# Reading the guard's flag behind the last store, and sending three of 24 stores in halves

## The chip, the core and the metric

The kernel runs on one core of a Trainium2 chip. The core has five engines with an instruction queue each: TensorE (PE, with its weight loads shown as PEld), VectorE (DVE), ScalarE (ACT), GpSimd (POOL) and SyncE (SP), which here issues all transfers. The metric is the time of one execution on the device in microseconds, taken from several runs by their median. The profile shows a single execution; its span goes from the first to the last instruction.

## What is computed

A gated linear attention over 4 batches, 8 heads, 768 positions and heads of 48, and a gated feed-forward part whose gate mixes the positions:

```python
f = 1 / (1 + exp(-f_logit))
for t in range(S):
    state = f[:, :, t, :, None] * state + einsum('bhd,bhe->bhde', k[:, :, t], v[:, :, t])
    y[:, :, t] = einsum('bhd,bhde->bhe', q[:, :, t], state)
x = y.transpose(0, 2, 1, 3).reshape(B, S, H * D)      # 4 x 768 x 384
h = gelu_tanh(x @ w_in)                               # 384 -> 1024
u, v = h[..., :512], h[..., 512:]
v_n = (v - mean) / sqrt(var + 1e-6) * g_ln
v_s = einsum('ts,bsd->btd', w_sg, v_n) + b_sg[None, :, None]
out = x + (u * v_s) @ w_out
```

All is float32. The result has 3072 rows of 384 numbers.

## The kernel before

The 3072 rows are cut into 24 tiles of 128 rows, six to a batch. For each tile the attention is computed in chunks of 64 positions, with the state carried along; then the tile goes through the first product, the GELU and the norm. The position mixing (`sgu`) runs over groups of three tiles, and behind it comes the product with `w_out` (`proj`), a residual addition on DVE (`residual`, L914) into a buffer of the ring `tmp`, and the store of the tile (`store`, L917), 128 rows of 1536 bytes.

A planner (`Plan.run`) puts all these steps into one order, from costs, due times and a list of shifts (`MOVES`), and the steps are then written out in this order under a manual schedule (L1169 to L1178). Each engine works through its own queue in that order. All transfers are issued by SP: the loads of f, k, q and v for a tile, the round trips through DRAM by which k and q are turned (`kq_d`, `raw`) and by which the decay goes to another layout (`dec_d`, `dec`), and the 24 stores. An issue that must wait holds up all that SP has behind it.

The transfers report through eight semaphores, which the framework hands out in rotation: each transfer takes the next, and is issued only when the one that had this semaphore eight transfers earlier has landed.

The fast path holds only for usual data. So the kernel collects flags (`guard`, `guard_sum`, `guard_end`), and a number `slow_i` says in the end whether a general path must run. Behind the last step every engine reads `slow_i` into a register (L1184) and branches (L1187). The general path is long, and is not entered with the data used here. Behind the branch stands a join, where SP waits for the eight semaphores of the transfers one after the other in a fixed order, and then the program closes (shown as L1283). At the step `ok_e`, L1178 marks a place for a branch hint on SP.

`store` is also called from the general path, where `row0` is a loop's register and not `None`.

Of the kernel before, what the change touches and what calls it, by code (L numbers as in the profile page):

```python
# [17 lines left out]
P = 128  # L18
C = 64
# [386 lines left out]
def gla_moe_kernel(ctx: ExitStack, tc: tile.TileContext, q, k, v, f, w_in, g_ln, w_sg, b_sg, w_out, cst, out):  # L406
    nc = tc.nc
# [72 lines left out]
    row0 = None  # L480
# [303 lines left out]
    out_flat = out.rearrange("b s e -> (b s) e")  # L784

    def out_rows(n):
        r = n * P if row0 is None else row0 + n * P
        return out_flat[ds(r, P), :]
# [121 lines left out]
    o_sb = {}  # L910
# [3 lines left out]
        nc.vector.tensor_add(o_sb[n], psum[f"po{n}"][:, :E], x_sb.pop(n))  # L914

    def store(n):
        nc.sync.dma_start(out_rows(n), o_sb.pop(n))  # L917

    slow_i = cp.tile([1, 1], mybir.dt.int32, name="slow_i")
    ok_t = {}  # L920
    last_sb = {}

    def guard():
        NG = 2 * N + N * 2 * NP
# [131 lines left out]
    for n in range(N):  # L1056
# [88 lines left out]
        if done:  # L1145
            plan.by[f"po{n}"]["needs"] += [f"po{n - 1}", f"po{n - 2}"]
        op(f"re{n}", lambda e, n=n: residual(n), T["re"], [f"po{n}"], take=("tmp",), unbank=f"po{n}", free=[("x", f"ty{n}", 0)])
        dma(f"out{n}", lambda e, n=n: store(n), W["out"], [f"re{n}"], free=[("tmp", f"re{n}", 0)])
    for n in range(NT, N):
        if n % NT == 0:  # L1150
# [30 lines left out]


    main.close()
    slow = nc.values_load(slow_i[0:1, 0:1], min_val=0, max_val=1)  # L1184

    table["set"] = "any"
    with tc.If(slow != 0, label="general"):  # L1187
# [27 lines left out]
        with tc.tile_pool(name="again", bufs=2) as wk, tc.tile_pool(name="ps_again", bufs=1, space=PSUM) as pp:  # L1215
# [4 lines left out]
            with tc.For_i(0, B * S, S) as row0:  # L1220
# [23 lines left out]
                for g in range(NT // GR):  # L1244
                    for ft in range(NF):
                        sums(f"sg{g}.{ft}")
                        sgu(g, ft)
                        sgu_bias(g, ft)
                        sgu_gate(g, ft, "POOL")
                        sgu_hi(g, ft)  # L1250
                        sgu_lo(g, ft)
                    for r in range(GR):
                        sums(f"po{g * GR + r}")
                        proj(g * GR + r)
                        residual(g * GR + r)
                        store(g * GR + r)
# [31 lines left out]
```

## Time and profile before

| | |
|---|---|
| median of 3 runs | 366.79 us (366.03 to 367.84) |
| the profiled execution | 365.51 us, span 363.7 us |
| mean granted TensorE clock | 0.997 |
| transfers | 45.89 MB, mean 126 GB/s |
| stores of results | 24, 192 KB each, all issued by SP |

The profiled execution is 1.28 us below the median of the three runs. In the rows of the profile a time such as 359.95 is counted from the start of the span. `SPq`, `PEldq` and the like are an engine's sequencer: waits, branches, register work and issues of transfers, which don't count as busy. For the issue of a transfer the row has the time that the issue took on SP, not the time until the data has landed. In a row of a line, "x4: 17/17/17, 360.8 to 361.1" is the count, the least, median and greatest duration in ns, and the start of the first and the last. In rows of waits the numbers are the total, the count and the longest, in us. In the table of stretches, the figures behind the stretch are its length, then the busy time (and count) of PE, PEld, DVE, ACT and POOL, the granted clock, the DMA share and GB/s.

### The profile page before, as it was taken

Reading aid. Unit: us, or ns where it says so; the run is one execution under the profiler, and the core shown is the slowest. Engines: PE = TensorE matmul, PEld = TensorE weight load, DVE = VectorE, ACT = ScalarE, POOL = GpSimd, SP = SyncE. Lnnn points to the kernel's source line nnn. Section 1 sums busy time; section 2 is a strip of 40 time slices with the busy share of each in tenths; the row PEclk is TensorE's granted clock in tenths of the full one; section 3 lists DMA queues with packets and bytes.
Section 4 is the critical chain, followed back from the end, with each engine's and each line's share of the span. In section 5 each row is a group of like instructions: output and inputs, shape, how many; then the busy total and the mean of one; then the engine's idle time right before and its main releaser. Section 6 shows DMA issues by size and latency. Waiting matters only on the chain.

```text
span 363.7 us, 11376 instructions
## 1 busy us (share of the span) xinstructions
PE 357.3 (98%) x4676; PEld 325.6 (90%) x4676; DVE 242.9 (67%) x561; ACT 241.0 (66%) x503; POOL 63.5 (17%) x113
## 2 busy tenths in 40 slices
PE   7999999999999999999999999999999999999995
PEld 3678788899999989899998999999998898999994
DVE  2999887788998966449765665255886944245532
ACT  5678999998658799798526674899424683811100
POOL 2211232322332201121002020130600010200100
PEclk9999999999999999999999999999999999999998
DMA  8999989425789778625744932035564720000012
GB/s 188 221 239 203 211 162 243 104 74 145 161 207 221 180 176 203 131 57 140 179 88 110 199 69 64 3 88 132 144 154 78 221 64 25 3 22 2 0 43 94
DMA packets 134046, 45.89 MB, mean 126 GB/s; under 512 B 117221, under 2 KB 130405, under 8 KB 133990
## 3 DMA queue, kind: packets, MB, share of 16 engines
q1 hardware_dynamic: 133990, 45.12, 53.3%
q8 instruction: 38, 0.62, 0.7%
q14 instruction: 18, 0.15, 0.1%
HBM read 33.25 MB, written 11.85 MB: 124 GB/s over the span
## 4 chain that ended last, share of the span: by engine, by line
PE 93%; DMA 3%; ACT 1%; SPq 1%; issue 0%; DVE 0%
PE ps_b L796 69%; PE ps_y L772 7%; PE ps_s L724 4%; PE ps_b L1168 3%; PE ps_s L729 2%; PE ps_b L801 2%; PE ps_b L679 2%; DMA cs<-in_consts_dram 2%; PE ps_b L664 1%; PE ps_b L627 1%; DMA vs<-in_v_dram 1%; PE ps_b L556 1%; PE ps_b L630 1%; PE ps_b L631 1%; SPq L500 0%
## 5 line engine op out<-in xcount | busy, mean ns | idle before, releaser
L796 PE MATMUL ps_b<-w_sg_hi,vh 128*128 128x384 f32 x192 | 65.6, 342 | 0.0
L796 PE MATMUL ps_b<-w_sg_hi,vh_lo 128*128 128x384 f32 x192 | 64.9, 338 | 0.0
L796 PE MATMUL ps_b<-w_sg_lo,vh 128*128 128x384 f32 x192 | 64.8, 338 | 0.0
L796 PE MATMUL ps_b<-w_out_hi,gg 128*128 128x384 f32 x174 | 48.3, 339 | 0.0
L428 ACT ACT_TABLE_LOAD x31 | 39.8, 1283 | 0.6
L796 PEld LDWEIGHTS ps_b<-w_sg_hi,vh 128*128 128x128 f32 x192 | 36.1, 188 | 0.2
L796 PEld LDWEIGHTS ps_b<-w_sg_lo,vh 128*128 128x128 f32 x192 | 36.1, 188 | 0.0
L796 PEld LDWEIGHTS ps_b<-w_sg_hi,vh_lo 128*128 128x128 f32 x192 | 36.0, 188 | 0.0
L796 PEld LDWEIGHTS ps_b<-w_out_hi,gg 128*128 128x128 f32 x174 | 31.7, 188 | 0.2
L883 DVE SCALAR_TENSOR_TENSOR tmp<-ps_b,cols,b_bc 128x384 f32<-128x384 f32 x32 | 19.6, 613 | 16.8 <-PE ps_b L796 16.7
L899 ACT CAST gg<-tmp 128x384 fp32r<-128x384 f32 x29 | 14.7, 512 | 24.0 <-DVE tmp L888 18.5
L796 PE MATMUL ps_b<-w_out_lo,gg 128*128 128x384 f32 x87 | 29.1, 335 | 0.0
L796 PE MATMUL ps_b<-xTh,w_in_hi 128*128 128x384 f32 x84 | 29.1, 347 | 0.0
L430 ACT ACTIVATE f<-f 128x384 f32<-128x384 f32 x48 | 25.3, 527 | 5.7 <-DMA f<-in_f_logit_dram 5.3
L856 DVE SCALAR_TENSOR_TENSOR vh_lo<-vg,vg_rs,vh 128x512 fp32r<-128x512 f32 x24 | 18.2, 759 | 15.4 <-ACT vh L851 15.2
L796 PE MATMUL ps_b<-xTh,w_in_lo 128*128 128x384 f32 x84 | 28.4, 338 | 0.0
L796 PE MATMUL ps_b<-xTl,w_in_hi 128*128 128x384 f32 x84 | 28.3, 337 | 0.0
L772 PEld LDWEIGHTS ps_y<-vs,st 64*64 64x64 f32 x768 | 24.5, 134 | 4.2 <-issue 3.6
L435 ACT COPY sk<-raw 112x512 f32<-112x512 f32 x27 | 16.2, 617 | 17.8 <-DMA raw<-kq_d 15.5
L772 PE MATMUL ps_y<-S,sk 48*64 48x48 f32 x768 | 27.2, 220 | 0.0
L772 PE MATMUL ps_y<-vs,st 64*64 64x48 f32 x768 | 27.2, 220 | 0.0
L796 PE MATMUL ps_b<-w_in_hi,xTh 128*128 128x512 f32 x63 | 25.7, 408 | 0.3 <-ACT u L430 0.2
(139 smaller groups left out, 883.9 us busy)
## 6 DMA issues: line engine op xcount, KB each, us to landing
kq_d<-gg SPq DMA_DIRECT2D x18, 384.0 KB
f<-in_f_logit_dram SPq DMA_DIRECT2D x24, 192.0 KB
kq<-in_q_dram SPq DMA_DIRECT2D x24, 192.0 KB
kq<-in_k_dram SPq DMA_DIRECT2D x24, 192.0 KB
vs<-in_v_dram SPq DMA_DIRECT2D x24, 192.0 KB
raw<-kq_d SPq DMA_DIRECT2D x36, 128.0 KB
out_dram<-tmp SPq DMA_DIRECT2D x24, 192.0 KB
gg<-in_moe_w_in_dram SPq DMA_DIRECT2D x8, 384.0 KB
```

What stands on the lines that cost most here:

```text
L428: nc.scalar.preload_act_table_set(SETS[want])
L430: nc.scalar.activation(dst, src, func, **kw)
L435: (nc.scalar.copy if e == "ACT" else ENG[e].tensor_copy)(dst, src)
L679: nc.tensor.transpose(psum[f"tr{n}"][j][:W2, p * P : (p + 1) * P], kq[:, j, 2 * p : 2 * p + 2, :].rearrange("t h d -> t (h d)")[:, :W2], i ...
L724: nc.tensor.matmul(ps_s[rows(score_rows(c, 2 * p + par)), par, p * C : (p + 1) * C], sk[r, 0, p, c], sk[r, 1, p, c], start=True, stop=True)
L729: nc.tensor.matmul(ps_s[feat(par), c, 256 + p * D : 256 + (p + 1) * D], kt[rows(c), h], vs[rows(c), h], start=True, stop=True)
L772: nc.tensor.matmul(ps_y[rows(c), half, h * D : (h + 1) * D], a, m, start=start, stop=stop)
L796: nc.tensor.matmul(ps, a, m, start=(j == 0), stop=(j == len(seq) - 1))
L856: nc.vector.scalar_tensor_tensor(vl, v_raw.pop(n), rs, vh.bitcast(F32), op0=ALU.mult, op1=ALU.subtract)
L883: nc.vector.scalar_tensor_tensor(t, psum[f"sg{g}.{ft}"][:, :E], g_col[:, ft : ft + 1], b_bc[:, tokens(g)], op0=ALU.mult, op1=ALU.add)
L899: nc.scalar.copy(gt[(g, ft)][0], g_raw[(g, ft)])
L1168: steps = plan.warm(plan.run(), 45.0, lambda k, n: nc.tensor.matmul(ps_b[k][:, : n * P], zeros, zeros[:, None, :].to_broadcast((P, n, P)), ...
```

## The change

Tiles 6, 7 and 8 are stored by two transfers of 64 rows each (`C` is 64), in place of one of 128 rows. All other stores stay, and the last one traced is kept in `last_store`. SP's instructions of the read of `slow_i` get an edge that orders them in SP's queue behind that store; it orders the issue and waits for no landing. The reads of the other engines are not touched.

```diff
     def store(n):
-        nc.sync.dma_start(out_rows(n), o_sb.pop(n))
+        o = o_sb.pop(n)
+        if row0 is None and n in (6, 7, 8):
+            nc.sync.dma_start(out_flat[n * P : n * P + C, :], o[:C])
+            nc.sync.dma_start(out_flat[n * P + C : (n + 1) * P, :], o[C:])
+        else:
+            last_store[0] = nc.sync.dma_start(out_rows(n), o)
...
-    last_sb = {}
+    last_sb, last_store = {}, [None]
...
     main.close()
-    slow = nc.values_load(slow_i[0:1, 0:1], min_val=0, max_val=1)
+    with tc.issue_after(last_store[0].ins):
+        slow = nc.values_load(slow_i[0:1, 0:1], min_val=0, max_val=1)
```

## Prediction

> **What bounds the kernel now.** I read the page first (span, busy times, chain), then the end of the run instruction by instruction: the timeline of SP, the chain of the last microseconds, and the views of lines 1184, 1187 and 1283, which hold the read of the flag, the branch with the join behind it, and the closing of the program. Last come the waits of SP, the stretches around the three split stores, and what PE waited for.
>
> ```profile
> span 363.7 us, 11376 instructions
> PE 357.3 (98%) x4676; PEld 325.6 (90%) x4676; DVE 242.9 (67%) x561; ACT 241.0 (66%) x503; POOL 63.5 (17%) x113
> PE 93%; DMA 3%; ACT 1%; SPq 1%; issue 0%; DVE 0%
> ```
>
> PE bounds the kernel up to its last product. The change adds no product and takes none away, so it can act in two places only: behind the last product, and where the extra store issues delay a load on which PE depends. The tail:
>
> ```profile
> 359.36 0.56 DVE tmp L914
> 356.10 0.33 SPq L917 DMA_DIRECT2D out_dram<-tmp  x1
> 357.83 0.34 SPq L917 DMA_DIRECT2D out_dram<-tmp  x1
> 359.95 0.33 SPq L917 DMA_DIRECT2D out_dram<-tmp  x1
> L1187 SPq COMPARE_BRANCH  x1: 70/70/70, 360.3 to 360.3; - x1
> L1187 SPq EVENT_SEMAPHORE  x4: 17/17/17, 360.8 to 361.1; - x4
> L1187 SPq EVENT_SEMAPHORE  x4: 17/17/17, 362.1 to 362.3; - x4
> SPq L1187 <- SPq L1187: 1.5, 2, 1.0
> L1283 SPq EVENT_SEMAPHORE  x8: 27/28/28, 362.4 to 362.9; - x8
> L1283 SPq DRAIN  x2: 7/10/13, 362.9 to 363.0; - x2
> L1283 PEldq DRAIN  x1: 8/8/8, 362.4 to 362.4; - x1
> ```
>
> The reader is to see one thread on SP. The last residual addition ends at 359.36 + 0.56 = 359.92; SP issues the last store at 359.95 and is free at 360.28; it branches at 360.3 and then waits for eight semaphores in turn. Four waits pass at once (360.8 to 361.1, so about 0.1 each). The fifth passes only at 362.1: this is the idle stretch of 1.0 in the row of SP's waits, and only the store issued at 359.95 can still be under way there, 2.15 us after its issue. The last three follow at 0.07 each, to 362.3. Eight closing waits (362.4 to 362.9) and the barrier to 363.7 come behind. So the end of the run is: landing of the last store, three more waits, closing. PE is through its own join at 362.4, some 0.6 before SP's drain at 363.0; that is the most that a quicker SP can gain before PE takes its place.
>
> **The change part by part.** *The semaphores.* The eight are handed out in rotation, and three halves are three more transfers. The last store moves from the fifth place of the wait order to the eighth. The three waits behind the landing go: 3 x 0.07 = 0.2 us off, if SP has the other seven waits behind it when the store lands at 362.1. Nothing else on SP covers those three waits now; they are on the path at full price.
>
> *The read of the flag.* In the profile it stands between two stores:
>
> ```profile
> L1184 SPq TENSOR_LOAD <-slow_i x1: 547/547/547, 356.5 to 356.5; - x1
> L1184 SPq FUSED_REGOPS  x1: 176/176/176, 357.1 to 357.1; - x1
> L1184 SPq SEQ_ASSERT  x1: 33/33/33, 357.3 to 357.3; - x1
> L917 SPq EVENT_SEMAPHORE  x1: 17/17/17, 357.4 to 357.4; - x1
> ```
>
> The store ahead of it is issued by 356.10 + 0.33 = 356.43 and the next instruction of SP starts at 357.4: the three instructions with their gaps take 0.97. There they cost nothing, because SP then waits until 357.83 for the next residual anyway; so taking them away there brings nothing either. No store is issued earlier by it. Behind the last store nothing stands beside them but that store's own flight. From 360.28 the branch now follows within about 0.04; in between go 0.97, so it moves by some 0.93, from 360.3 to 361.25, and the first wait from 360.8 to 361.73. Queued behind the read on SP are only the branch, the join and the closing; the other engines read the flag for themselves and don't wait for SP before the closing barrier.
>
> Seven steps at 0.07 to 0.1 bring SP from the first wait to the eighth: 0.5 to 0.7, and by the mixture of the rows (three at 0.1, four at 0.07) 0.58. The eighth then passes at 361.73 + 0.58 = 362.3, within 0.1. Before, the eighth passed at 362.3 too. The store has landed by 362.1, so nothing waits for it any more: SP's own string of instructions has become the bound, and the 0.2 that the rotation gives is used up by the 0.93 that the read takes. The landing itself could come sooner or later by 0.1 or 0.2 and change nothing. Sum at the end: 0.0, bounds -0.2 (the read entirely hidden) and +0.2 (steps of 0.1 throughout and rounding).
>
> The Trainium skill, "Runtime: NRT & Kernel Launch", section "The ~15µs preamble/postamble breakdown", gives about 1.3 us for a TENSOR_LOAD, there from HBM. By that figure the eighth wait would come 0.75 later, at 363.05, and the sum would be +0.75. The trace has 547 ns for this very instruction, reading the on-chip flag, and that decides.
>
> *The halves.* Three more issues on SP, each 0.36 (rows below) plus about 0.04 of gap, 0.4 with its wait; a half has half of the partitions, and I give it the whole price, since the trace has no half store. The bytes stay. Around them:
>
> ```profile
> 191.40 2.44 SPq L917 DMA_DIRECT2D out_dram<-tmp  x2
> 193.94 0.39 SPq L592 DMA_DIRECT2D vs<-in_v_dram  x1
> 194.87 0.39 SPq L589 DMA_DIRECT2D kq<-in_k_dram  x1
> 199.76 0.35 SPq L917 DMA_DIRECT2D out_dram<-tmp  x1
> 200.20 0.39 SPq L586 DMA_DIRECT2D f<-in_f_logit_dram  x1
> 202.50 1.20 SPq L592 DMA_DIRECT2D vs<-in_v_dram  x1
> 205.57 2.03 SPq L704 DMA_DIRECT2D raw<-kq_d  x4
> 212.92 0.39 SPq L592 DMA_DIRECT2D vs<-in_v_dram  x1
> 197.92 0.26 DVE L435 COPY vs<-vs 64x192 f32<-64x192 f32 x1 [0.28 <-DMA vs<-in_v_dram]
> 206.59 0.25 DVE L435 COPY vs<-vs 64x192 f32<-64x192 f32 x1 [0.52 <-DMA vs<-in_v_dram]
> 208.95 0.62 DVE L883 SCALAR_TENSOR_TENSOR tmp<-ps_b,cols,b_bc 128x384 f32<-128x384 f32 x1 [0.34 <-PE ps_b L796]
> 213.15 0.13 PE ps_s L724 x8
> 195.00:200.00 5.00, 5.00 (x43) 4.33 (x44) 4.42 (x12) 4.63 (x7) 2.43 (x3) 1.00 0.64 123
> 205.00:210.00 5.00, 5.00 (x32) 4.97 (x31) 3.05 (x6) 2.54 (x8) 1.37 (x4) 1.00 0.95 185
> PEld ps_s L724 <- DVE tmp L914: 0.4, 1, 0.4
> ```
>
> Stores 6 and 7 are the two of 191.40. The first ends at 191.76 and the second starts at 193.48, so the extra half of store 6 lies in idle time. That of store 7 pushes the load of v from 193.94 to 194.34; the load of k behind it had waited until 194.87, with 0.5 of room, so the push ends there. The half of store 8 pushes everything from 200.20 to the last turned piece at 207.6 by 0.4; then SP is idle until 212.92. The turned pieces feed products that PE starts at 213.15, microseconds later. The two pushed loads of v end waits of DVE (197.92, 206.59). So DVE runs up to 0.4 late twice; the second time it has 0.34 of idle time at 208.95 to give. PE itself is busy for 5.00 of 5.00 us in both stretches, and the one pause of its weight loads put down to DVE is that of 0.4, at the scores behind store 8. I cost the halves at 0, hidden by PE's queue of products; if this cover fails, each push costs PE 0.4 at most. A transfer also waits for the one eight places before it; with three more in the rotation some wait for one that is up to three places nearer. Those are some 5 us old or more when asked for (a store issued at 199.76 is asked for by the transfers just ahead of 205.57), against 2.15 for a store from issue to landing and 4.1 for the load of v at 202.50, which DVE reads at 206.59; I take 0.
>
> **Sum.** 0.0 at the end, 0.0 in the middle: the profiled execution, 365.51 with a span of 363.7, would come out at 365.5. The median of the runs shown is 366.79, 1.28 above; the same sum on the median gives 366.8, and I write 366.7 because the cheaper end of the tail is nearer to the rows than the dearer one.
>
> **The rivals.** *First, the 0.2 stays.* The rotation pays in full if the first seven waits are done by 362.1. From the first wait to the eighth are 0.58, so the first must be at 361.5 or earlier: the read may cost 0.7, not 0.93. A quicker read behind a drained queue, or a scheduler that leaves the read where it is so that only the rotation changes, would do it. For it: the bare read is 0.55 of the 0.97. Against it: the gaps stood in the same place, directly behind a store's issue. Time 366.79 - 0.2 = 366.6.
>
> *Second, the halves reach PE*: 0.4 once, since PE has no idle time later to give it back: 367.2. For it: the pause of 0.4 that ends with DVE's residual, which the first pushed load of v delays. Against: DVE's room, and that one push must find a product that waits for exactly that engine.
>
> *Third, the other side: SP's branch finds its code absent.*
>
> ```profile
> L1187 PEldq COMPARE_BRANCH  x1: 3734/3734/3734, 358.4 to 358.4; - x1
> L1187 DVEq COMPARE_BRANCH  x1: 72/72/72, 360.0 to 360.0; - x1
> ```
>
> PE's branch over the general path takes 3734 ns, those of DVE and SP about 70. Line 1178 marks a hint for SP alone. The halves bring three issues with their waits, so SP's branch stands some six instructions further on in its code, and the read stands between the last store and the branch. If SP then pays what PE pays, its first wait moves by 3.66 more, and it decides from the first nanosecond, as SP is last already: 366.8 + 3.7 = 370.5. Against it: the hint stays, and DVE passes without one. The Trainium skill, "Runtime: NRT & Kernel Launch", section "Instruction fetch mechanics", says that a taken branch to code outside the two resident pages stalls until that page is fetched. PE's row agrees with it, the rows of DVE and SP show no such stall; which pages SP holds, no view shows.
>
> **How the numbers follow.** No change at the end and in the middle 0.52 (366.7); the 0.2 stays 0.20 (366.6); the halves reach PE 0.14 (367.2); the missing code 0.08 (370.5); something that no row shows 0.06, shared by both sides. A measurement of this kernel can tell about 0.5% from no change, that is 1.8 us. No case reaches that on the fast side: PE's join leaves 0.6 at most. So faster 0.04, same 0.85, slower 0.11. The first three cases lie between 366.6 and 367.2; the three runs shown lie from 366.03 to 367.84, so the range goes from 365.7 to 367.9 and leaves the missing code out.
>
> **What would show it.** In the profile after: the read of line 1184 on SP behind the last store, at about 360.3; the branch at 361.2 or 361.3; all eight waits of line 1187 evenly from about 361.7 to 362.3, none of them with an idle 1.0. If seven pass early and the eighth stands alone at 362.1, the first rival holds. A branch of SP of microseconds is the third. If the last residual ends later than 359.92 against the start, look for the 0.4 at the scores near 200. I am wrong altogether if the span moves by over a microsecond with the tail as described.

## The result, and the profile after: 1% slower

| | before | after |
|---|---|---|
| median | 366.02 us (365.55 to 367.84) | 370.12 us (369.24 to 371.12) |
| ratio | | 1.0105, 95% interval 1.0078 to 1.0131 |
| the profiled execution, span | 363.7 us | 368.4 us |
| the last residual ends | 359.92 | 362.48 |
| from there to the end of the span | 3.82 | 5.92 |

No change was forecast; the kernel became 4.1 us slower. The profiled spans differ by 4.66, in two places: the last residual addition ends 2.56 later, and the stretch behind it is 2.10 longer. The page of the changed kernel: span, busy times, code transfers (queue, packets, MB, share of the DMA engines) and the chain that ended last.

```profile
span 368.4 us, 11377 instructions
PE 357.8 (97%) x4676; PEld 325.6 (88%) x4676; DVE 242.7 (66%) x561; ACT 240.6 (65%) x503; POOL 64.4 (17%) x113
q14 instruction: 19, 0.16, 0.1%
PE 84%; DMA 5%; SPq 4%; ACT 3%; DVE 2%; issue 1%; DVEq 0%; ACTq 0%
```

The same page of the kernel before has one transfer of code fewer on that queue:

```profile
q14 instruction: 18, 0.15, 0.1%
```

PE is no busier than before (357.8 against 357.3 us), and its share of the chain fell from 93% to 84%; DMA, SP, ACT and DVE took the rest. That one transfer of code more, 18 to 19, is easily passed over; it turns out to be the sign of the larger part. The lines of the tail after:

```profile
L914 DVE TENSOR_TENSOR tmp<-ps_b,x x6: 535/558/559, 351.3 to 361.9; 128x384 f32<-128x384 f32 x6
L922 SPq DMA_DIRECT2D out_dram<-tmp x6: 332/332/333, 351.9 to 362.5; - x6
L1190 SPq TENSOR_LOAD <-slow_i x1: 561/561/561, 362.9 to 362.9; - x1
L1190 SPq SEQ_ASSERT  x1: 37/37/37, 363.7 to 363.7; - x1
L1193 SPq COMPARE_BRANCH  x1: 70/70/70, 364.2 to 364.2; - x1
L1193 SPq EVENT_SEMAPHORE  x8: 17/17/17, 366.5 to 367.0; - x8
L1193 PEldq COMPARE_BRANCH  x1: 3417/3417/3417, 361.0 to 361.0; - x1
L1289 SPq EVENT_SEMAPHORE  x10: 17/28/28, 367.1 to 368.3; - x10
```

And the row of SP's waits:

```profile
SPq L1193 <- SPq L1193: 2.2, 1, 2.2
```

The last store goes at 362.5, the read follows at 362.9 and ends with its assertion at 363.78. Then two things are new. The branch starts 0.39 later, where the instruction before it had been followed after 0.05; and the first of the eight waits comes 2.29 after the branch, where it was 0.51. The branch itself shows 70 ns, as before: the stall stands as the idle 2.2 between the branch and the line's next instruction. The last store had landed at 364.59 in the trace, so the waits then pass evenly (366.46 to 367.01) with no landing among them.

The middle, in SP's timeline after (start, duration, instruction):

```profile
193.69 0.47 SPq L919 DMA_DIRECT2D out_dram<-tmp  x1
194.20 0.60 SPq L920 DMA_DIRECT2D out_dram<-tmp  x1
194.89 2.27 SPq L592 DMA_DIRECT2D vs<-in_v_dram  x1
197.27 0.53 SPq L589 DMA_DIRECT2D kq<-in_k_dram  x1
...
202.52 0.49 SPq L919 DMA_DIRECT2D out_dram<-tmp  x1
203.07 0.59 SPq L920 DMA_DIRECT2D out_dram<-tmp  x1
203.75 0.54 SPq L586 DMA_DIRECT2D f<-in_f_logit_dram  x1
...
208.50 3.48 SPq L704 DMA_DIRECT2D raw<-kq_d  x4
```

A half takes 0.47 to 0.60, more than a whole store's 0.36, and a load behind the halves takes 0.53 to 0.54 instead of 0.39. So a split holds SP 0.7 to 0.8 longer. The load of v, pushed from 193.94 to 194.89, takes 2.27 instead of 0.39. What DVE makes of that, in its timeline after:

```profile
199.88 0.26 DVE L435 COPY vs<-vs 64x192 f32<-64x192 f32 x1 [2.03 <-DMA vs<-in_v_dram]
200.16 0.58 DVE L649 TENSOR_TENSOR kq<-kq,eb 128x384 f32<-128x384 f32 x1
200.67 1.35 DVE L903 TENSOR_TENSOR gg<-tmp,gg 128x384 fp32r<-128x384 f32 x1
201.95 0.55 DVE L914 TENSOR_TENSOR tmp<-ps_b,x 128x384 f32<-128x384 f32 x1
```

POOL's product of k (L644) after, and the same pair of DVE and POOL before:

```profile
200.42 1.20 POOL L644 TENSOR_TENSOR kq<-kq,f 128x384 f32<-128x384 f32 x1
```

```profile
198.72 0.55 DVE L903 TENSOR_TENSOR gg<-tmp,gg 128x384 fp32r<-128x384 f32 x1
198.96 1.18 POOL L644 TENSOR_TENSOR kq<-kq,f 128x384 f32<-128x384 f32 x1 [0.57 <-ACT f L430]
```

The copy of v waits 2.03 for the load and starts 1.96 later than before (199.88 against 197.92). L903 then takes 1.35 instead of 0.55. The two products overlap before as well; but there DVE's starts first, by 0.24, and now POOL's does, by 0.25. It is the order that goes with the price: of the eighteen profiled executions behind this document, the six in which POOL's starts first (0.08 to 0.26 ahead) have 1.35 to 1.37 for L903, and the other twelve 0.54 to 0.55. Both together make the residual of tile 8, and with it store 8, late by 2.76 (202.52 against 199.76). Behind it all loads are late, and so are the four issues of `raw`, by 2.9 (208.50 against 205.57), which also take 3.48 instead of 2.03. The view of waits from 205 to 220 closes the chain:

```profile
PEld ps_s L724 <- ACT sk L435: 1.9, 1, 1.9
PE ps_s L724 <- ACT sk L435: 1.8, 1, 1.8
DVE sk L435 <- DMA raw<-kq_d: 1.7, 1, 1.7
ACT sk L435 <- DMA raw<-kq_d: 1.2, 1, 1.2
```

None of the four stands in that view of before. ACT's copy of the turned pieces, first before and then after:

```profile
210.61 0.61 ACT L435 COPY sk<-raw 112x512 f32<-112x512 f32 x1
```

```profile
214.49 0.62 ACT L435 COPY sk<-raw 112x512 f32<-112x512 f32 x1 [1.17 <-DMA raw<-kq_d]
```

Before, PE's scores (L724) started at 212.97, 1.75 after the copy's end. Now PE stands still until the copy's end. Matmul against matmul, PE's lateness jumps there by 1.98, and once more by 0.57 at 302.5 (L772). This second jump doesn't belong to the change: it is 0.27 in e5_pad3, whose executed program is that of before, and 0.55 in e12_late_old_drain, which has no half ahead of it.

### The profile page after: what moved, and what is told of

It is laid out like the page before. It is cut to its first block, busy times and chain, and to the rows that moved or that the text cites. A ratio compares the mean times of both kernels' runs of the same rounds, so it can differ in the third digit from the quotient of the medians.

```text
span 368.4 us, 11377 instructions
## 1 busy us (share of the span) xinstructions
PE 357.8 (97%) x4676; PEld 325.6 (88%) x4676; DVE 242.7 (66%) x561; ACT 240.6 (65%) x503; POOL 64.4 (17%) x113
## 4 chain that ended last, share of the span: by engine, by line
PE 84%; DMA 5%; SPq 4%; ACT 3%; DVE 2%; issue 1%; DVEq 0%; ACTq 0%
PE ps_b L796 64%; PE ps_y L772 6%; PE ps_s L724 4%; PE ps_s L729 2%; PE ps_b L801 2%; DMA f<-in_f_logit_dram 2%; PE ps_b L1173 2%; DMA vs<-in_v_dram 1%; PE ps_b L556 1%; SPq L586 1%; PE ps_b L679 1%; PE ps_b L630 1%; SPq L500 1%; PE ps_b L664 1%; SPq L589 1%; PE ps_b L631 1%
## 5 line engine op out<-in xcount | busy, mean ns | idle before, releaser
L772 PEld LDWEIGHTS ps_y<-vs,st 64*64 64x64 f32 x768 | 24.5, 134 | 4.2 <-issue 2.8
L772 PE MATMUL ps_y<-S,sk 48*64 48x48 f32 x768 | 27.2, 220 | 0.6 <-issue 0.6
L772 PE MATMUL ps_y<-vs,st 64*64 64x48 f32 x768 | 27.2, 220 | 0.0
```

The lines of the kernel that those rows point to most:

```text
L772: nc.tensor.matmul(ps_y[rows(c), half, h * D : (h + 1) * D], a, m, start=start, stop=stop)
```

## The experiments

Each kernel was timed beside the kernel before on the same chip. "Tail" is the time from the end of the last residual to the end of the span (before: 3.82); "stall" is the time from the start of SP's branch to the first wait behind it (before: 0.51); "place" counts SP's traced instructions up to the branch, from 0; "step" is PE's jump at the scores near 213 against the trace of before. All of the profiled execution, in us.

| | ratio (95%) | place | code transfers on q14 | stall | tail | step |
|---|---|---|---|---|---|---|
| before | | 460 | 18 | 0.51 | 3.82 | |
| after | 1.0105 (1.0078 to 1.0131) | 463 | 19 | 2.29 | 5.92 | 1.98 |
| e1_read_only | 1.0015 (0.9992 to 1.0037) | 460 | 18 | 0.51 | 3.78 | 0 |
| e2_halves_only | 1.0060 (1.0028 to 1.0093) | 463 | 19 | 2.53 | 5.22 | 1.14 |
| e3_late_halves | 1.0053 (1.0036 to 1.0071) | 464 | 19 | 2.22 | 5.84 | 0 |
| e4_short_general | 1.0089 (1.0072 to 1.0105) | 463 | 19 | 2.38 | 6.01 | 1.40 |
| e5_pad3 | 1.0006 (0.9991 to 1.0022) | 460 | 18 | 0.51 | 3.75 | 0 |
| e6_late_pad | 1.0068 (1.0037 to 1.0100) | 464 | 19 | 2.22 | 5.84 | 0 |
| e7_late_pad_old | 1.0000 (0.9983 to 1.0017) | 464 | 19 | 0.62 | 3.54 | 0 |
| e8_split7 | 1.0102 (1.0070 to 1.0134) | 463 | 19 | 2.45 | 6.08 | 0.38 |
| e9_split8 | 1.0064 (1.0041 to 1.0086) | 463 | 19 | 2.32 | 5.95 | 0.85 |
| e10_drain3 | 1.0046 (1.0023 to 1.0070) | 463 | 19 | 2.56 | 5.24 | 0 |
| e11_late_drain | 0.9997 (0.9977 to 1.0018) | 488 | 19 | 0.54 | 3.80 | 0 |
| e12_late_old_drain | 1.0009 (0.9988 to 1.0031) | 488 | 19 | 0.54 | 3.50 | 0 |
| e13_delay | 1.0019 (0.9992 to 1.0047) | 484 | 19 | 0.53 | 3.73 | 0.54 |
| e14_change_drain | 1.0009 (0.9982 to 1.0035) | 487 | 19 | 0.54 | 3.80 | 0.78 |
| e15_change_again | 1.0085 (1.0059 to 1.0111) | 463 | 19 | 2.28 | 5.91 | 0.58 |
| e16_halves_drain | 0.9996 (0.9982 to 1.0009) | 487 | 19 | 0.54 | 3.52 | 1.57 |

### The two parts of the change, each alone

e1_read_only keeps all stores whole:

```diff
-        if row0 is None and n in (6, 7, 8):
+        if row0 is None and n in ():
```

> All 24 stores whole, so the semaphores rotate as before; only SP's read of the flag stands behind the last store. Theory A (code position: SP's three more issues push the code behind the general path out of the block that SP holds): the issues are as many as before, so the branch reaches its first wait about 0.5 us after it starts, as before; last residual at about 360, end of the span 3.8 us behind it, time within 0.3 us of before. Rival B (the read just ahead of the branch makes the branch slow): the first wait comes 2.3 us after the branch, and the tail is about 5.9 us, time +2.1 us.

e2_halves_only puts the read back to its old place:

```diff
-    with tc.issue_after(last_store[0].ins):
-        slow = nc.values_load(slow_i[0:1, 0:1], min_val=0, max_val=1)
+    slow = nc.values_load(slow_i[0:1, 0:1], min_val=0, max_val=1)
```

> Stores 6, 7 and 8 in halves, the read where it was before. Theory A: three more issues, so the branch still costs some 2 us more than before, though the read is far from it; the tail is 5 to 5.3 us. Rival B: the branch costs 0.5 us as before, the tail is 3.6 us. Middle: if the halves delay the loads behind them (and not the moved read), PE's scores near 213 still come 2 us late and the last residual ends at about 362.4.

The line of the branch and the join in e1_read_only:

```profile
L1193 SPq EVENT_SEMAPHORE  x8: 17/17/17, 361.3 to 361.8; - x8
L1193 SPq COMPARE_BRANCH  x1: 70/70/70, 360.8 to 360.8; - x1
```

The moved read alone costs nothing that can be measured, and its branch is quick: 360.8 to 361.3. With the halves alone the branch stalls as in the whole change, and a step in the middle is there, of 1.14 where about 2 was expected. So both losses come with the halves. The rival by which a read just ahead of the branch slows it falls.

### The halves elsewhere

e3_late_halves splits 17, 18 and 19; e8_split7 and e9_split8 leave one of the early splits and move the other two:

```diff
-        if row0 is None and n in (6, 7, 8):
+        if row0 is None and n in (17, 18, 19):      # e3_late_halves
+        if row0 is None and n in (7, 18, 19):       # e8_split7
+        if row0 is None and n in (8, 18, 19):       # e9_split8
```

> The change with stores 17, 18 and 19 in halves, behind which SP has no loads, in place of 6, 7 and 8. Middle: the last residual ends at about 360 as before, so 2 to 2.6 us of the loss are gone. Theory A: as many issues as in the change, so the tail stays at 5.9 us and the time is about 2 us above before. If the slow branch came from the lateness of the loads, the tail would be 3.8 us and the time that of before.

> The change with stores 7, 18 and 19 in halves in place of 6, 7 and 8. If store 7's second half starts the loss by delaying the load of v behind it, DVE's copy of v at 198 comes 0.7 us later, DVE then meets POOL's multiplication of k, store 8 leaves 1.4 us later, the turned pieces some 1 us later, and of that 0 to 0.5 us reach PE's scores near 213 (in the change 1.1 to 2.0 in three profiles). If the loss is store 8's, PE loses nothing here. The tail is slow as in the change (5.9 us).

> The change with the halves at stores 8, 18 and 19. If the step of PE at the scores near 213 starts with the half of store 7 and that of store 8 only adds what it pushes itself, this kernel has 0 to 0.3 us of it (the split of 7 alone had 0.38, all three 1.98). If store 8's half is the one that matters, 1.0 us or more. The tail is that of the change, 5.8 to 6.1 us behind the last residual, since SP issues as many instructions.

With late halves the step is gone and the tail is not: 5.84. The two losses are separate, and the tail doesn't ask which stores are split. Store 7's split alone has a step of 0.38. That of 8 alone has 0.85, between the 0 to 0.3 that was expected and the 1.0 or more of its rival: store 8's half doesn't only add to a delay that store 7's brought, it makes its own. In SP's timeline of e9_split8 behind the two halves:

```profile
201.22 0.53 SPq L586 DMA_DIRECT2D f<-in_f_logit_dram  x1
201.85 1.96 SPq L656 DMA_DIRECT2D dec<-dec_d  x1
```

This single issue of `dec` took 0.69 in the trace of before. From 201.68, 0.17 ahead of it, a code transfer of 1.61 us runs on queue q8. I take the transfers of this queue for PE's code, since one starts in each trace within PE's branch of 3.3 to 3.8.

### What the tail depends on

Three theories were open: the place to which SP's branch leads, the number of transfers in the rotation, and the place of the branch in SP's own code. e4_short_general shifts what lies between the branch and its target by leaving three of the four result transfers of each turn out of the general path, which doesn't run here:

```diff
-                for b in range(B):
+                for b in range(1):
                     nc.sync.dma_start(xd[
```

> The change, with three of the four result transfers in the general path's first loop left out (that path isn't entered with these data), so that SP's code between branch and join is at least six instructions shorter. Theory A: the target of the branch comes back into the block that SP holds; the first wait comes 0.5 us after the branch and the tail is about 3.8 us, with the middle as slow as in the change: time about 2 us above before and 2 us under the change. If the branch is slow because the branch itself, not its target, has crossed into another block, or because of the read ahead of it, the tail stays at 5.9 us.

The stall stays (2.38, tail 6.01), where the first theory had expected 0.5 and 3.8: making the skipped path shorter by these transfers changes nothing. e5_pad3, e6_late_pad and e7_late_pad_old were meant to shift SP's code by empty instructions behind store 16 (three in the kernel before; sixteen with late halves, in the last one with the read in its old place):

```diff
+        if row0 is None and n == 16:
+            for _ in range(3):
+                nc.sync.nop(nofuse=True)
```

> The kernel before, with three empty instructions in SP's queue behind store 16, where SP has nothing to do for some 15 us; nothing else differs. Theory C (SP fetches its code in blocks; the block behind the branch is fetched only when SP enters the block that holds the branch, and before the change the branch stood as one of the last instructions of a block): three more instructions put the branch at the head of the next block, and it waits for the fetch: the first wait comes 2.2 to 2.6 us after the branch, the tail from the last residual to the end of the span is 5.2 us in place of 3.8, the time 1.4 us above before. If the semaphores' rotation, the halves or the read make the branch slow, the tail is 3.8 us and the time that of before.

> Stores 17, 18 and 19 in halves, the read behind the last store, and 16 empty instructions on SP behind store 16. Theory C: SP enters the new block some eight microseconds ahead of the branch, so the fetch is over when it is needed: first wait 0.5 us after the branch, tail 3.8 us, eight waits with no idle time among them, time within 0.3 us of before. If any shift of the code makes the branch slow, the tail is 5.2 to 5.9 us.

> As the one with late halves and 16 empty instructions, but with the read where it was before the change. The rotation alone is left: seven waits pass early, the eighth ends with the last store's landing, tail 3.6 us, that is 0.2 us less than before; time 0.2 us under before, too little to tell by its interval.

The empty instructions are not in the executions: the place of the branch is 460 and 464 as without them. e5_pad3 is thus the kernel before once more and tells nothing of the theories, and e6_late_pad repeats e3_late_halves. e7_late_pad_old is a kernel of its own all the same, with late halves and the old read. It has the branch at place 464, behind the boundary, and yet a stall of 0.62. There place 463 is the issue of the last store, for which SP stands waiting from 2.1 ahead of the branch; the boundary is crossed before that wait. And with the read out of the way the rotation pays: seven waits pass early, the eighth at 361.56, 0.02 after the last landing, and the tail is 3.54, 0.28 less than before.

Drains do stand in the trace. e10_drain3 is the kernel before with three of them, e11_late_drain and e12_late_old_drain have 24 with late halves (read behind the last store, and in its old place):

```diff
+        if row0 is None and n == 16:
+            for _ in range(3):
+                nc.sync.drain()
```

> The kernel before with three empty instructions (drains) on SP behind store 16, and nothing else: no half, the read where it was. Theory of the code block: SP's branch moves from the place 460 of its executed instructions to 463, behind the boundary at 462/463, and its first wait comes 2.2 to 2.6 us behind it instead of 0.5; the time from the last residual to the end goes from 3.8 to about 5.2, and the whole from 366.0 to 367.4. Rival, that halves or the moved read slow the branch by themselves: first wait 0.5 us behind the branch, no change of the time. The middle has no step in either case.

> Halves at stores 17, 18 and 19, the read behind the last store, and 24 drains on SP behind store 16. Theory of the code block: the boundary now lies some 26 instructions ahead of the branch, its fetch runs while SP waits for a residual, and the branch takes 0.5 us to the first wait; behind the last residual 3.6 to 3.9 us instead of the 5.84 without the drains; time within 0.2 of the kernel before. Rival, that three more issues or the read slow the branch at whatever place: 5.8 us as without the drains, and 1.6 us more than the kernel before.

> As the last, with the read of the flag in its old place: only the rotation and the 24 drains differ from the kernel before. The rotation's own gain stays: seven waits pass before the last store lands, the eighth with it; behind the last residual 3.5 us instead of 3.8, the whole 0.2 to 0.3 us shorter than the kernel before, a ratio of 0.9990 to 1.0. [...]

e10_drain3 has neither a half nor a moved read. Its page, the line of its branch, and its row of SP's waits:

```profile
q14 instruction: 19, 0.16, 0.1%
```

```profile
L1190 SPq EVENT_SEMAPHORE  x8: 17/17/17, 363.4 to 363.9; - x8
L1190 SPq COMPARE_BRANCH  x1: 70/70/70, 360.8 to 360.8; - x1
```

```profile
SPq L1190 <- SPq L1190: 2.5, 1, 2.5
```

Three drains of 139 ns together, 60 us ahead of the branch, make it stall 2.56 and the kernel 0.46% slower, without anything of the change: no transfer more in the rotation, no moved read. Its tail of 5.24 is that of e2_halves_only (5.22), 1.42 longer than before. The other 0.68 of the changed kernel's 2.10 come with the moved read, which puts off the branch and with it the stall, and has no wait for a landing left to stand beside. And in e11_late_drain, which has the late halves and the moved read, 24 drains take it away:

```profile
L1196 SPq EVENT_SEMAPHORE  x8: 17/17/17, 362.7 to 363.3; - x8
L1196 SPq COMPARE_BRANCH  x1: 70/70/70, 362.2 to 362.2; - x1
```

The boundary can be seen there, among its drains (the two stretches from 301.5 to 303.25 and from 303.25 to 304):

```profile
L925 SPq DRAIN  x18: 7/7/123, 302.2 to 303.2; - x18
```

```profile
L925 SPq DRAIN  x6: 7/7/136, 303.6 to 304.0; - x6
```

Drains follow each other every 0.05, but between the 18th and the 19th, places 462 and 463, lie 0.37. That is the gap that stands right ahead of the branch in e10_drain3 (0.38) and in the changed kernel (0.39). The theory holds in all eighteen executions: where SP goes past place 462 ahead of its branch, the page counts 19 transfers of code on q14, otherwise 18; and where the branch is the first or the second instruction behind it, following at once, it stalls 2.2 to 2.6. From the end of instruction 462 to the first wait the changed kernel takes 2.68, e10_drain3 2.94. In the changed kernel a q14 transfer starts at 364.82, 1.04 after instruction 462, and ends at 365.18, 1.28 ahead of the first wait.

The traces show two things more. In all fifteen executions that go past place 462 a q14 transfer starts 1.01 to 1.06 after the end of instruction 462, also where the branch is 59 us away (e11_late_drain, 1.02). So it is the crossing that goes with this transfer and not the branch, and the kernels that stall have no transfer more than those that cross early: 19 in both. And in the nine that stall the first wait comes 2.67 to 2.94 after instruction 462, whether the branch is the first behind it or, as in e3_late_halves (2.70), the second. In e7_late_pad_old it comes 2.73 after, and its stall of 0.62 fits this: the 2.1 that SP spent waiting for the residual had used up nearly all. So what the branch pays is what is left of some 2.7 us when SP reaches it. That SP waits there for the transfer is inferred from these times; what the transfer carries, no view shows.

e12_late_old_drain has the tail of 3.50 that was expected, but its time isn't distinguishable from the kernel before; the 0.3 of the rotation is smaller than what these runs can resolve.

### What the middle depends on

e13_delay holds SP behind stores 7 and 8 without any half; e14_change_drain is the whole change with 24 drains behind store 16, e16_halves_drain the same with the old read; e15_change_again is the changed kernel once more.

```diff
+        if row0 is None and n in (7, 8):            # e13_delay, in the kernel before
+            for _ in range(12):
+                nc.sync.drain()
```

> The kernel before with twelve drains on SP behind store 7 and twelve behind store 8, no half and no moved read. Twelve drains hold SP for some 0.7 us (125 ns and eleven at 52), as long as one split does. Theory of SP's time: what SP issues behind them is late by about 0.7 at either place, the issues meet PE's code transfer near 195 and 202 otherwise than before, and PE has a step of 0.4 to 2.0 us at the scores near 213. Rival, that the two transfers of 64 partitions themselves (their packets, their semaphores) make the delay: 0 to 0.2 us. The branch stands 24 places further on and is quick (0.5 us to the first wait), the tail 3.8 us in either case.

> The whole change (halves 6, 7 and 8, the read behind the last store) with 24 drains on SP behind store 16. By the code block the tail goes back to 3.8 us behind the last residual, the middle keeps its step of 1.1 to 2.0 us at the scores near 213 (2.6 with the later one near 302): 367.0 to 368.5 us, a ratio of 1.003 to 1.007. If the middle of the changed kernel were a chance of its one profile, the ratio is 1.000.

> The changed kernel unaltered, timed on one chip together with the next kernel, so that its middle can be told from its end. The end costs 2.0 to 2.1 us by its two profiles. If the middle costs 0.3 to 1.0 in the usual execution, as the kernel with drains had it, the changed kernel is 2.3 to 3.1 us above the one before (1.006 to 1.0085), and the 2.0 of its profile was one execution's high value; if the middle costs 2, it is 4.1 us above (1.011).

> Halves 6, 7 and 8, the read in its old place, 24 drains behind store 16: what is left against the kernel before is the rotation (0.2 to 0.3 us less at the end, seven waits early and the eighth with the last landing, 3.5 us behind the last residual) and the middle. With a middle of 0.3 to 1.0 the ratio is 1.0000 to 1.002; with one of 2 us it is 1.0045 or more.

The delay alone, in e13_delay's view of waits from 205 to 221, gives the same wait at the same scores:

```profile
PEld ps_s L724 <- ACT sk L435: 0.5, 1, 0.5
PE ps_s L724 <- ACT sk L435: 0.4, 1, 0.4
```

So SP's time is enough to make a step at these scores; the half transfers are not needed for one. Its 0.54 is at the low end of the 0.4 to 2.0 that was expected. e14_change_drain, with 0.78, missed the 1.1 to 2.0 expected of it, and e15_change_again has 0.58. SP's timeline of e15_change_again, the same program as the changed kernel, shows what differs from one execution to the next:

```profile
194.52 0.54 SPq L592 DMA_DIRECT2D vs<-in_v_dram  x1
195.16 1.55 SPq L589 DMA_DIRECT2D kq<-in_k_dram  x1
```

A transfer of PE's code starts at 194.95 here. The issue that follows, of k, takes 1.55; that of v is through in 0.54. In the changed kernel's first profile the transfer starts at 194.99 and the load of v, issued 0.10 ahead of it, takes 2.27. DVE needs v first, and k only behind it. In the six executions with halves 6, 7 and 8 the steps sort by this: 1.98 and 1.57 where v was hit (after, e16_halves_drain), 0.58 to 1.40 where k or q was hit. It isn't the only thing that differs. In e15_change_again DVE's L903 takes 0.55, in the other five 1.35 to 1.36; and in e4_short_general, whose step is 1.40, another transfer on q8 meets the second half of store 8, which takes 1.47. What each of the three is worth, six executions can't tell. In the kernel before q is hit, and costs nothing:

```profile
195.31 1.39 SPq L589 DMA_DIRECT2D kq<-in_q_dram  x1
```

In time the middle is smaller than in the first profile. e14_change_drain expected 1.003 to 1.007 and came to 1.0009, e16_halves_drain to 0.9996, though its own profile has a step of 1.57. The changed kernel timed again is at 1.0085, 3.1 us, of which the tail is 2.1. By the four timings the middle costs between nothing and 1.7 us (1.0105 x 366 less 366 and the 2.1); e2_halves_only and e4_short_general, counted in the same way, give 0.8 and 1.1. Its usual value within that is not settled.

## Why the prediction was wrong, step by step

**The step that failed** is the one at the end: "From 360.28 the branch now follows within about 0.04", and with it "the first wait from 360.8 to 361.73". It took the 0.51 from branch to first wait as a fixed price of this branch. It is the price of a branch that SP reaches well behind or ahead of a crossing. With three issues more the branch moved to the first place behind a boundary, and its price became 0.39 + 2.29 instead of 0.05 + 0.51: 2.1 more, all of it on the path. The rival of the missing code named this, with a chance of 0.08 and a price of 3.7. It was right about the place of the branch in SP's code, which is three instructions further on and not some six; the moved read, which it named beside the place, isn't needed (e10_drain3). Its price was PE's, and SP's is lower. What was held against it, that the hint stays and DVE passes, decided nothing: DVE's branch takes 72 ns in the changed kernel too. The Trainium skill, "Runtime: NRT & Kernel Launch", section "Instruction fetch mechanics", says that crossing a block of code is mostly hidden and that a taken branch outside the held pages stalls. The runs agree with the first: the crossing of e11_late_drain among its drains, 59 us ahead of the branch, cost 0.37 and no time at the end. For the second they show the stall, 2.56 in e10_drain3, but no transfer for the branch's target: the count is 19 in both kernels, and the transfer comes with the crossing.

**The read's price and the rotation** were right. Where the branch is quick, the moved read puts the first wait 1.88 after the residual (e11_late_drain; forecast 361.73 - 359.92 = 1.81), and the eighth 2.42 after it (forecast 2.38), so the tail stays as it was, at 3.80. The rotation alone makes the tail 0.28 to 0.32 shorter than that of before (e7_late_pad_old, e12_late_old_drain) where 0.2 was worked out: the store's landing no longer has the three waits behind it, and the rest is within the scatter of the tails (3.73 to 3.82 for those with nothing of the change in them). So "sum at the end: 0.0" holds for these two parts; the third part was missing.

**The halves** were costed at 0, "0.4 with its wait" hidden by PE's queue. Two sizes were off. A split costs SP 0.7 to 0.8, not 0.4: both halves are dearer than the whole, and so is the load behind them. And the push doesn't stay what it is: the issue near 195 us that ran beside a transfer on q8 took 1.2 to 2.3 us in every execution, and L903 0.8 more behind the start of POOL's product, so that a push of under 1 us became 2.76 at store 8 in the first profile. The room ahead of the scores, 1.75 us by ACT's copy, was not worked out at all; "microseconds later" stood in its place. That cover is used up in each of the six profiled executions with halves 6, 7 and 8, and in the median costs less than the first profile shows. The rotation as such, costed at 0 in the middle, isn't tested there, since the late halves come behind it; e13_delay, which has no transfer more, shows that a step of 0.54 needs no rotation.

**What was to show it** was named well: the waits come evenly with no landing among them, as forecast, only 4.7 later than forecast against the start; and the microseconds at the branch stand not in its own duration, where PE's had them, but in the idle time behind it. The scores to look at were those near 213, not near 200.

## What to carry to other kernels

An edit that adds a few instructions to a queue moves everything behind them in that engine's code; where the queue ends in a branch on the critical path, compare the count of code transfers on the page before and after, and the time from the branch to the next instruction, not the branch's own duration. Where that costs, drains ahead in the queue, at a spot where the engine waits anyway, can take the boundary away from the branch. Their number matters: here 24 did it, and three, in the kernel before, brought the boundary to the branch. And an extra issue in a loaded stretch can cost more than its own duration, through what it pushes: here a load that got slow beside a code transfer, and a product of DVE that came to start behind POOL's. Work out the room of the last consumer before calling it hidden.

## What the runs showed of the hardware

- On SP a store of 64 partitions took 0.47 to 0.60 us to issue in the changed kernel, one of 128 partitions at the same places before 0.35 to 0.36, and a load behind the halves 0.53 to 0.54 instead of 0.39.
- In each of the eighteen executions, the code transfer on q8 near 195 us goes with one long issue on SP: 1.2 to 2.3 us, where the other loads beside it took 0.4 to 0.7.
- A crossing in SP's code showed 0.36 to 0.39 us of gap and one transfer more on q14 (0.16 MB in 19 transfers, 8 KB each), which started 1.01 to 1.06 us after the last instruction ahead of it; a branch right behind it had its next instruction 2.2 to 2.6 us later, 2.67 to 2.94 after that last instruction, and one behind a crossing long past 0.5.
- A drain on SP took 7 ns and came every 0.05 us, the first behind an issue 0.12.
- DVE's product L903 (128x384) took 1.35 to 1.37 us when POOL's product L644 had started 0.08 to 0.26 ahead of it, and 0.54 to 0.55 when DVE's started first or at the same time, though the two overlapped in both cases (eighteen executions).
